# The last two blocks of a fused attention and gated feed-forward kernel: row groups, tokens on partitions, and the casts of the first batch

## The chip, the cores and the metric

The kernel runs on one NeuronCore of one Trainium2 chip. The metric is the time of one execution on the device, in microseconds; the median of three runs is 719.71 us (718.67 to 720.09). The profile is of one execution, with a span of 716.4 us on the core.

Five engines work side by side, each through its own queue in order: TensorE (PE, with its weight loads shown as PEld), VectorE (DVE), ScalarE (ACT), GpSimd (POOL) and SyncE (SP), which here issues the transfers. PE writes its results to PSUM[...]; VectorE and ScalarE read them from there.

## The reference

Four batches of 12416 tokens of 128 channels pass through attention over 32 inducing points, and every token of the result through a gated feed-forward layer with 1536 hidden channels.

```python
def mab(q, kv):
    s = scale * (q @ kv.transpose(0, 2, 1))
    s = s - s.max(-1, keepdims=True)
    a = np.exp(s)
    a /= a.sum(-1, keepdims=True) + 1e-09
    return a @ kv
h = mab(I, x)          # 32 inducing points look at all tokens of the batch
out = mab(x, h)        # each token looks at the 32 points

gate = np.maximum(out @ w_gate, 0.0)
val = out @ w_val
return gate * val @ w_out
```

## The kernel before

Tokens lie as 97 tiles of 128 (`t`) of a batch; a block is four tiles (512 tokens), a pair two blocks, and one tile is left as the rest. `h` never meets the tokens as such: `hgv` holds `h @ w_gate` on partitions 0 to 63 (the 32 rows twice) and `h @ w_val` on 64 to 127, and the unnormalised scores `p2` (exp of the scores, 32 rows per block) multiply it. The sum of the scores is divided out once at the end, squared (`z2i` twice), since gate and value both carry it and the rectifier doesn't mind a positive factor.

A unit is one step of one pair. In a slot of the main loop PE forms the values of an older unit and the gates of the new one, ScalarE rectifies the gates (two of 128x512), VectorE multiplies gate and value (`gv`, one of 128x1024), and PE adds some output steps of a block whose `gv` is done. A pair has 12 units; output jobs stand in a queue, each with a first slot and a count of steps for each of its slots.

```python
    while True:
        unit = next(todo_units, None)
        window.append(unit)
        ready = None if at == 10 else window.pop(0)     # the lag grows by one here
        ...
        def values():
            ready["v"] = bank("v", "v_ps", [P, 2 * BLK])
            for m in ready["mm"][1]:
                form(ready["v"], *m)                     # L830, 32-row matmuls
        if ready and at >= 10:
            values()
        if unit:
            ... gates, L830 ...
        if ready and at < 10:
            values()
        ... posted work, a filler if due, output steps (L640, L696) ...
        if at < 10:
            idle(idle_ps, 2, hgv[:, 0:BLK])
        ... relu on ScalarE (L930), gate * value on VectorE (L933) ...
        at += 1
```

An output step of a regular block has the weights `wo` stationary and 512 tokens moving, so the result has channels on partitions; it is cast to fp16 (L646), transposed by a transfer and scaled on GpSimd (L657). The last two blocks are done otherwise, as the transfer would come too late:

```python
        def step(i):                                     # L696
            nc.tensor.matmul(c["ps"], wo[:, i, :], gv(i), start=(i == 0), stop=(i == NFF - 1))
        def evac(at):
            ... zz = z * z on VectorE (L701) ...
            for a in (0, h):                             # L705
                nc.scalar.copy(out=oT[:, a * P : (a + h) * P], in_=c["ps"][:, a * P : (a + h) * P])
            extra[at + 1].append(lambda: finish(zz, oT, osb))
        def finish(zz, oT, osb):
            for a in (0, h):
                ... transposes on PE (L712), scaling by zz on ScalarE (L716, first block)
                ... or VectorE (L720, last block), store (L727)
```

In the last pair one block's gates use one row group and its values another:

```python
    for r in (32 * k, 64 + 32 * k)     # gates, values of block k; two matmuls each on the same rows
```

The head, for the first batch, takes x in parts of eight tiles (two of four at the end):

```python
    for j in range(n_parts + 3):
        if j < n_parts:                                  # cast to fp16
            h = (t1 - t0) // 2
            nc.gpsimd.tensor_copy(out=dst[:, 0:h, :], in_=x32[:, 0:h, :])       # L283
            nc.scalar.copy(out=dst[:, h:, :], in_=x32[:, h:, :])                # L284
        if 1 < j < n_parts + 2:
            ... scores of part j - 2 on PE (L289), exp on ScalarE (L291)
        if j > 2:
            if j == n_parts + 2:
                nc.tensor.matmul(z1, ones32[0:1, :], z1s[0:1, :], start=False, stop=False)  # L298
            ... sums z1 and hT of part j - 3 on PE (L300, L310, L313)
        if j < n_parts:
            ... transposes of part j on PE (L318), copy to xT on VectorE (L319)
    ... weights cast on GpSimd (L327)
    idle(idle_ps, 3, xT[0][:, 0:4, :].rearrange("p t c -> p (t c)"))            # L272
    hT = finish_h(hT_ps, z1)           # reciprocal L142, product L144 on VectorE
    ... scores of the first pair (L175), hgv (L156, L335, L340), then the main loop
```

`idle` issues matmuls whose results nobody reads.

Of the kernel before, what the change touches and what calls it, by code (L numbers as in the profile page):

```python
# [18 lines left out]
def kernel(  # L19
# [16 lines left out]
    nc = tc.nc  # L36
# [135 lines left out]
    def s2_pair_pe(hT, xT, pr):  # L172
        ps = bank("g", "s2_ps")
        for r in range(4):
            nc.tensor.matmul(  # L175
                ps[32 * r : 32 * r + 32, :],
                hT[:, 0:M],
                xTs(xT, (2 * pr + r % 2) * TPB, TPB),
                start=True,
                stop=True,  # L180
            )
        return ps

    def s2_pair_exp(ps):
        p2 = st([P, BLK], FP16, "p2", 4)
        nc.scalar.activation(out=p2, in_=ps, func=AF.Exp, scale=sm_scale)
        return p2

    def s2_quad_pe(hT, xT, qd):

        ps = bank("g", "s2_ps")
        for r in range(4):
            nc.tensor.matmul(  # L193
                ps[32 * r : 32 * r + 32, :],
                hT[:, 0:M],
                xTs(xT, (4 * qd + r) * TPB, TPB),
                start=True,
                stop=True,
            )
        return ps  # L200
# [6 lines left out]
    def p2_copies(p2q):  # L207

        p2 = [st([P, BLK], FP16, "p2", 4) for _ in range(2)]
# [57 lines left out]
    n_big = n_parts - 2  # L267

# [5 lines left out]
    for j in range(n_parts + 3):  # L274
        if j < n_parts:
# [3 lines left out]
            if t1 == NT:  # L279
                nc.vector.tensor_copy(out=dst, in_=x32)  # L280
            else:
                h = (t1 - t0) // 2
                nc.gpsimd.tensor_copy(out=dst[:, 0:h, :], in_=x32[:, 0:h, :])  # L283
                nc.scalar.copy(out=dst[:, h:, :], in_=x32[:, h:, :])  # L284
# [9 lines left out]
        if j > 2:  # L294
            t0, t1 = parts[j - 3]
            p1, n = p1s[j - 3], t1 - t0
            if j == n_parts + 2:
                nc.tensor.matmul(z1, ones32[0:1, :], z1s[0:1, :], start=False, stop=False)  # L298
            if j - 3 < n_big:
# [31 lines left out]
    s2 = s2_pair_pe(hT, xT, 0)  # L331
    p2 = s2_pair_exp(s2)
# [6 lines left out]
    for k in (1, 2):  # L339
# [33 lines left out]
    def ev_s2_pair(b, pr, first, last):  # L373
        def pe(at):
            ps = s2_pair_pe(state[b]["hT"], state[b]["xT"], pr)

            def act():
                p2s[(b, pr)] = s2_pair_exp(ps)

            post[at + 1].append(act)  # L380
            ev_z2(lambda: p2s[(b, pr)], [(b, pr, k) for k in range(2)], TPB, at + 2)
# [3 lines left out]
    def ev_s2_quad(b, qd, first, last):  # L385
        def pe(at):
            ps = s2_quad_pe(state[b]["hT"], state[b]["xT"], qd)
# [71 lines left out]
    for b in range(B):  # L459
        for qd in range(NPAIR // 2):  # L460
            base = slot(b, 2 * qd, 0)
            if base:

                a = base - 2 * NFF if qd else slot(b - 1, NPAIR, 0) - 14
                ev_s2_quad(b, qd, a + 4, a + 8)
            else:
                ev_s2_pair(b, 1, 5, 8)
# [165 lines left out]
    def chain(w, gv, key, k, t0, first):  # L633
# [43 lines left out]
        if w == BLK:  # L677
            steps = [(first if i == 0 else 0, lambda i=i: step(i)) for i in range(NFF)]
            fast = key[0] == B - 1 and key[1] > NPAIR - 5
            counts = (5, 5) if fast else (6, 5)  # L680
# [6 lines left out]
    extra = defaultdict(list)  # L687

    def last_block(gv, key, k, t0, tag, on_act):
        c = {}  # L690
        h = TPB // 2

        def step(i):
            if i == 0:
                c["ps"] = bank(tag, "o_ps")
            nc.tensor.matmul(c["ps"], wo[:, i, :], gv(i), start=(i == 0), stop=(i == NFF - 1))  # L696

        def evac(at):
            z = z2is[key + (k,)][:, :, 0]
            zz = st([P, TPB], FP32, "zz", 2)  # L700
            nc.vector.tensor_tensor(out=zz, in0=z, in1=z, op=ALU.mult)  # L701
            oT = st([P, BLK], FP16, "oT", 4)
            osb = st([P, TPB, P], FP32, "osb", 4)
            for a in (0, h):
                nc.scalar.copy(out=oT[:, a * P : (a + h) * P], in_=c["ps"][:, a * P : (a + h) * P])  # L705
            extra[at + 1].append(lambda: finish(zz, oT, osb))

        def finish(zz, oT, osb):
            for a in (0, h):
                ps = bank("g", "oo_ps", [P, h, P], FP16)  # L710
                for t in range(h):
                    nc.tensor.transpose(ps[:, t, :], oT[:, (a + t) * P : (a + t + 1) * P], eye16)  # L712
                for t in range(h):
                    sc = zz[:, a + t : a + t + 1]
                    if on_act:
                        nc.scalar.activation(  # L716
# [250 lines left out]
```

The softmax here doesn't subtract the row's maximum and nothing guards it: scores larger than these inputs give would overflow.

## Time and profile before

| what | from the profile |
|---|---|
| span | 716.4 us |
| first gate product of VectorE | starts at 28.67 us |
| last gate product of VectorE | ends at 710.50 us |
| last matmul of an output step | ends at 711.60 us |
| last scaling on VectorE | ends at 713.57 us |

In a list in order of time a row has the start, the duration of what is merged in it, the engine, the line of the kernel, the operation, output and inputs by name, shapes, and a count; brackets tell how long the engine was idle before it and what ended that. Rows of the same kind that follow each other are merged, so the pace of a merged row is its duration less one instruction's, divided by the count less one. A PE row's duration includes the time until its last result is there. The page also gives, by stretches of time, the busy time of each engine and the TensorE clock that was granted.

### The profile page before, as it was taken

What the parts mean: (1) busy time and instruction counts of PE and PEld (TensorE: products, weight loads), DVE (VectorE), ACT (ScalarE), POOL (GpSimd) and SP (SyncE); (2) the same over time, 40 slices, a digit from 0 to 9 for tenths busy, and PEclk for the clock granted to TensorE, in tenths of its full rate; (3) what the DMA queues carried; (4) which work ended last, traced back from release to release, by engine and by line L of the source; (5) the groups of instructions that cost most, each with busy time, mean ns of one, the idle gap of its engine ahead of it and who ended that gap; (6) DMA issues with size and microseconds to landing.
All of it is one profiled execution on the core that took longest, in us unless ns stands there. A gap on an engine that the chain in (4) does not pass through costs nothing.

```text
span 716.4 us, 13907 instructions
## 1 busy us (share of the span) xinstructions
PE 639.5 (89%) x4554; PEld 191.1 (27%) x4554; DVE 684.5 (96%) x630; ACT 679.6 (95%) x1378; POOL 343.3 (48%) x621
## 2 busy tenths in 40 slices
PE   5999999998988999998898999999888898898997
PEld 5422222222222222222222222222222222222222
DVE  4699999999999999999999999999999999999996
ACT  5799999999999999999999999999999999999985
POOL 3574536561365546626163662754325451551531
PEclk9999999999999999999999999999999999999999
DMA  9656677531346978522147766762122133232222
GB/s 344 219 125 177 150 181 163 103 89 45 91 126 166 195 164 223 126 67 76 46 107 206 170 155 170 170 118 75 59 68 83 56 90 67 67 88 67 67 68 72
DMA packets 142489, 87.76 MB, mean 122 GB/s; under 512 B 116913, under 2 KB 125905, under 8 KB 140113
## 3 DMA queue, kind: packets, MB, share of 16 engines
q1 hardware_dynamic: 142416, 86.88, 46.8%
q8 instruction: 35, 0.57, 0.3%
q14 instruction: 38, 0.30, 0.1%
HBM read 27.80 MB, written 25.43 MB: 74 GB/s over the span
## 4 chain that ended last, share of the span: by engine, by line
PE 44%; ACT 23%; issue 15%; DVE 15%; DMA 3%; SPq 0%; POOL 0%; DVEq 0%; ACTq 0%
PE o_ps L640 19%; ACT g L930 16%; DVE gv L933 14%; PE v_ps L830 14%; PE g_ps L830 7%; ACT oT L646 6%; DMA gv<-in_x_dram 2%; PE s_ps L193 1%; PE o_ps L696 1%; PE s1T_ps L511 1%; ACT p1T L521 0%; PE idle_ps L272 0%; DMA p1g<-p1T 0%; ACT hgv L166 0%; PE xT_ps L318 0%
## 5 line engine op out<-in xcount | busy, mean ns | idle before, releaser
L933 DVE TENSOR_TENSOR gv<-g,v_ps 128x1024 f16<-128x1024 f16 x576 | 660.8, 1213 | 10.7 <-PE g_ps L830 6.8
L930 ACT ACTIVATE g<-g_ps 128x512 f16<-128x512 f32 x1164 | 613.3, 620 | 16.6 <-PE g_ps L830 8.6
L640 PE MATMUL o_ps<-gv,wo 128*128 128x512 f16 x1128 | 339.8, 383 | 36.8 <-ACT oT L646 36.6
L657 POOL TENSOR_SCALAR osb<-o,z2i 128x128 f32<-128x128 f16 x380 | 164.6, 447 | 275.0 <-DMA o<-oT 251.3
L830 PE MATMUL g_ps<-p,hgv 32*128 32x512 f16 x1152 | 284.8, 380 | 5.3 <-ACT g L930 1.7
L830 PE MATMUL v_ps<-p,hgv 32*128 32x512 f16 x1152 | 226.2, 383 | 11.5 <-DVE gv L933 9.7
L830 PEld LDWEIGHTS <-hgv 32*128 32x128 f16 x2400 | 73.6, 91 | 271.5 <-issue 267.3
L640 PEld LDWEIGHTS <-wo 128*128 128x128 f16 x1176 | 79.2, 97 | 192.0 <-issue 169.1
L436 POOL TENSOR_TENSOR z2i<-zt,minus 128x16 f32<-128x16 f32 (+2 forms) x29 | 72.5, 2501 | 1.5
L646 ACT CAST oT<-o_ps 128x512 f16<-128x512 f32 (+1 forms) x98 | 57.1, 583 | 0.4 <-PE o_ps L640 0.4
L490 POOL CAST x<-x 128x2048 f16<-128x2048 f32 x18 | 34.0, 1890 | 19.4 <-DMA x<-in_x_dram 15.0
L429 POOL TENSOR_TENSOR zt<-zt 128x128 f32<-128x128 f32 (+5 forms) x116 | 33.4, 288 | 9.1
L595 POOL TENSOR_TENSOR hp<-hp,hq 128x129 f32<-128x129 f32 (+1 forms) x18 | 8.2, 457 | 32.5 <-ACT hq L594 27.9
L429 POOL TENSOR_TENSOR zt<-p2T 128x256 f32<-128x256 f16 (+2 forms) x29 | 17.0, 586 | 9.3 <-DMA p2T<-p2q 7.0
L319 DVE COPY xT<-xT_ps 128x1024 f16<-128x1024 f16 (+1 forms) x13 | 8.5, 650 | 7.2 <-PE xT_ps L318 6.4
L204 ACT ACTIVATE p2q<-s_ps 128x512 f16<-128x512 f32 x23 | 15.1, 656 | 0.0
L283 POOL CAST x<-gv 128x512 f16<-128x512 f32 (+1 forms) x13 | 7.5, 580 | 12.3 <-DMA gv<-in_x_dram 12.2
L284 ACT CAST x<-gv 128x512 f16<-128x512 f32 (+1 forms) x13 | 7.5, 580 | 6.1 <-DMA gv<-in_x_dram 6.1
L521 ACT ACTIVATE p1T<-s1T_ps 128x512 f16<-128x512 f32 x18 | 12.2, 677 | 0.0
L318 PE MATMUL xT_ps<-eye,x 128*128 128x128 f16 x97 | 9.6, 256 | 2.1 <-POOL x L283 1.5
L193 PE MATMUL s_ps<-xT,hT 128*32 128x512 f16 x92 | 9.2, 387 | 1.9
L291 ACT ACTIVATE p<-s_ps 128x256 f16<-128x256 f32 (+2 forms) x14 | 5.0, 354 | 4.9 <-PE s_ps L289 4.8
(90 smaller groups left out, 162.1 us busy)
## 6 DMA issues: line engine op xcount, KB each, us to landing
out_dram<-osb SPq DMA_DIRECT2D x94, 256.0 KB, 2.2
x<-in_x_dram SPq DMA_DIRECT2D x18, 1024.0 KB, 5.8
p<-p2q SPq DMA_DIRECT2D x92, 64.0 KB, 2.0
gv<-in_x_dram SPq DMA_DIRECT2D x11, 512.0 KB, 7.5
o<-oT SPq DMA_TRANSPOSE x98, 2.3
x<-in_moe_w_out_dram SPq DMA_DIRECT2D x1, 768.0 KB, 9.1
gv<-in_x_dram SPq DMA_DIRECT2D x2, 256.0 KB, 10.7
x<-in_moe_w_gate_dram SPq DMA_DIRECT2D x1, 512.0 KB, 9.2
```

What stands on the lines that cost most here:

```text
L193: nc.tensor.matmul(ps[32 * r : 32 * r + 32, :], hT[:, 0:M], xTs(xT, (4 * qd + r) * TPB, TPB), start=True, stop=True,)
L204: nc.scalar.activation(out=p2q, in_=ps, func=AF.Exp, scale=sm_scale)
L429: nc.gpsimd.tensor_tensor(out=dst, in0=v[:, :, :, 0:m], in1=v[:, :, :, m : 2 * m], op=ALU.add)
L436: nc.gpsimd.tensor_tensor(out=z2i, in0=v[:, :, :, 0], in1=minus1[:, 0 : n * g].rearrange("p (n g) -> p n g", n=n), op=ALU.pow,)
L490: nc.gpsimd.tensor_copy(out=s["x16"][:, t0:t1, :], in_=s["x32", q])
L521: nc.scalar.activation(out=p1T, in_=ps, func=AF.Exp, scale=sm_scale)
L640: nc.tensor.matmul(c["ps"][:, 0:w], wo[:, i, :], gv(i), start=(i == 0), stop=(i == NFF - 1))
L646: nc.scalar.copy(out=oT[:, 0:w], in_=c["ps"][:, 0:w])
L657: nc.gpsimd.tensor_scalar(out=osb[:, t, :], in0=o16[:, t, :], scalar1=zz, scalar2=zz, op0=ALU.mult, op1=ALU.mult,)
L830: nc.tensor.matmul(ps[:, cols], hgv[:, s * P : (s + 1) * P], p2, start=True, stop=True)
L930: nc.scalar.activation(out=g16[:, k * BLK : (k + 1) * BLK], in_=ps, func=AF.Relu)
L933: nc.vector.tensor_tensor(out=ready["dst"], in0=ready["g16"][:, 0:n], in1=ready["v"][:, 0:n], op=ALU.mult)
```

## The change

Most of it is for the last pair. All four row groups are used at once: gates of both halves on groups 0 and 1, values on 2 and 3. For that each of the last two blocks gets scores of its own in all four groups, and the pair before gets its scores directly rather than by copies between partitions. The output steps put the tokens on partitions, with `gv` stationary and `wo` moving, so no transpose is needed; four such groups share a bank, which a matmul of zeros opens. The last block is scaled by VectorE straight from PSUM, the one before by GpSimd after a copy by ScalarE. The last gate product is split in two.

```diff
+                if b == B - 1 and qd == NPAIR // 2 - 1:
+                    bl = 2 * NPAIR - 4
+                    ev_s2(b, (b, 2 * qd), (bl, bl + 1, bl, bl + 1), a + 4, a + 8)
+                    for k in range(2):
+                        ev_s2(b, (b, 2 * qd + 1, k), (bl + 2 + k,) * 4, a + 16 + 6 * k, a + 20 + 6 * k)
+                else:
+                    ev_s2_quad(b, qd, a + 4, a + 8)
...
-            counts = (5, 5) if fast else (6, 5)
+            counts = (6, 5)
+            if fast:
+                counts = (4, 4) if (key[1], k) == (NPAIR - 2, 1) else (5, 5)
...
         def step(i):
             if i == 0:
-                c["ps"] = bank(tag, "o_ps")
-            nc.tensor.matmul(c["ps"], wo[:, i, :], gv(i), start=(i == 0), stop=(i == NFF - 1))
+                ps = bank("o", "o_ps")
+                nc.tensor.matmul(ps, zero16, wo[0:1, 0:TPB, :], start=True, stop=False)
+                c["ps"] = ps.rearrange("p (t c) -> p t c", t=TPB)
+            for t in range(TPB):
+                nc.tensor.matmul(
+                    c["ps"][:, t, :],
+                    gv(i)[:, t * P : (t + 1) * P],
+                    wo[:, i, :],
+                    start=False,
+                    stop=(i == NFF - 1 and t == TPB - 1),
+                )
 
         def evac(at):
...
+            if last:
+                h = TPB // 2
+                for a in (0, h):
+                    nc.vector.tensor_tensor(
+                        out=osb[:, a : a + h, :],
+                        in0=c["ps"][:, a : a + h, :],
+                        in1=zz[0][:, a : a + h, :].broadcast_to([P, h, P]),
+                        op=ALU.mult,
+                    )
+                    nc.sync.dma_start(
+                        out=ov[key[0]][:, t0 + a : t0 + a + h, :], in_=osb[:, a : a + h, :]
+                    )
+                return
+            o32 = st([P, TPB, P], FP32, "o32", 1)
+            nc.scalar.copy(out=o32, in_=c["ps"])
+            for t in range(TPB):
+                nc.gpsimd.tensor_scalar(...)
...
-                        if k == 0:
-                            steps = [(base + 8, lambda i=i, f=step: f(i)) for i in range(NFF)]
-                            job(steps, evac, ([3, 3, 3, 3],) * 2)
-                        else:
-                            for i in range(NFF):
-                                a = base + 12 + (i + 2) // 4
-                                extra[a].append(lambda i=i, f=step: f(i))
-                            extra[base + 15].append(lambda f=evac: f(base + 16))
+                            lambda i, k=k: base + 3 + 6 * k + i // 2,      # first slot of step i
+                        job(steps, evac, ([1, 3, 3, 3, 3] if k == 0 else [0] + [4] * 8,) * 2)
...
-                                    for d in range(2)
+                                    for d, r in ((0, 64 * j), (1, 64 * j + 32))
                                 ]
-                                for r in (32 * k, 64 + 32 * k)
+                                for j in range(2)
                             ],
                             dst=gvs[k][:, u % 6, :, :].rearrange("p k c -> p (k c)"),
+                            parts=2 if u == NFF - 1 else 1,
```

The rest is for the head. A full part of x is cast whole by one engine, in turn; only the last part is still shared. Three idle matmuls are added ahead of the last part's sums, to keep PE in work. The lag of the main loop grows at slot 4, and values come ahead of gates throughout. Buffers for `p2` go from four to five, and each of the second and third copies of `hgv` is issued beside its matmuls.

```diff
+            elif j == n_parts - 1:
+                nc.gpsimd.tensor_copy(out=dst[:, 0:2, :], in_=x32[:, 0:2, :])
+                nc.scalar.copy(out=dst[:, 2:4, :], in_=x32[:, 2:4, :])
             else:
-                h = (t1 - t0) // 2
-                nc.gpsimd.tensor_copy(out=dst[:, 0:h, :], in_=x32[:, 0:h, :])
-                nc.scalar.copy(out=dst[:, h:, :], in_=x32[:, h:, :])
+                if on_act:
+                    nc.scalar.copy(out=dst, in_=x32)
+                else:
+                    nc.gpsimd.tensor_copy(out=dst, in_=x32)
+                on_act = not on_act
...
                 nc.tensor.matmul(z1, ones32[0:1, :], z1s[0:1, :], start=False, stop=False)
+                idle(idle_ps, 3, xT[0][:, 0:4, :].rearrange("p t c -> p (t c)"))
...
-        ready = None if at == 10 else window.pop(0)
+        ready = None if at == 4 else window.pop(0)
```

## The prediction

> **What bounds the kernel now.** I read the page's busy times first, then the engines' busy time by stretches, then VectorE alone in order of time, and last the order of time of all engines at the two ends, because the change touches only the first 30 us, a few scores at slots 541 to 563, and the last 20 us.
>
> ```profile
> PE 639.5 (89%) x4554; PEld 191.1 (27%) x4554; DVE 684.5 (96%) x630; ACT 679.6 (95%) x1378; POOL 343.3 (48%) x621
> ```
>
> VectorE (DVE) and ScalarE (ACT) are both nearly full. VectorE alone, late in the last batch:
>
> ```profile
> 638.99 53.25 DVE L933 TENSOR_TENSOR gv<-g,v_ps 128x1024 f16<-128x1024 f16 x47
> ```
>
> 47 gate products without a pause: one lasts 1.22 us and they start every (53.25 - 1.22) / 46 = 1.131 us, so their rate is the floor of a slot here. In batches 0 to 2 six slots take about 7.07 us (the ScalarE evacuations of `oT` at 51.00, 58.06, 65.13) and ScalarE shows almost no pause, so there it sets the rate and VectorE has 7.07 - 6 x 1.131 = 0.28 us in six slots to spare.
>
> PE in that part, one slot from 663.25 to 664.33, and PE, VectorE, ScalarE and the store queue in the last 12 units:
>
> ```profile
> 663.25 0.39 PE L830 MATMUL v_ps<-p,hgv 32*128 32x512 f16 x2
> ...
> 663.58 0.82 PE L640 MATMUL o_ps<-gv,wo 128*128 128x512 f16 x3
> 664.33 0.39 PE L830 MATMUL v_ps<-p,hgv 32*128 32x512 f16 x2
> ```
>
> ```profile
> 695.16 8.75 DVE L933 TENSOR_TENSOR gv<-g,v_ps 128x1024 f16<-128x1024 f16 x7 [0.78 <-ACT g L930]
> ...
> 706.14 0.38 PE L830 MATMUL v_ps<-p,hgv 32*128 32x512 f16 x1
> 706.15 0.38 PE L830 MATMUL g_ps<-p,hgv 32*128 32x512 f16 x1
> 706.37 0.37 PE L830 MATMUL v_ps<-p,hgv 32*128 32x512 f16 x1
> 706.38 0.37 PE L830 MATMUL g_ps<-p,hgv 32*128 32x512 f16 x1
> ...
> 706.68 0.82 PE L696 MATMUL o_ps<-gv,wo 128*128 128x512 f16 x3
> ...
> 710.14 1.46 PE L696 MATMUL o_ps<-gv,wo 128*128 128x512 f16 x6
> ...
> 712.44 1.13 DVE L720 TENSOR_SCALAR osb<-oo_ps,zz 128x128 f32<-128x128 f16 x4 [1.87 <-PE oo_ps L712]
> 713.08 0.85 SPq L727 DMA_DIRECT2D out_dram<-osb  x2
> ```
>
> A regular slot with three output steps takes PE 664.33 - 663.25 = 1.08 us, one of the last units 1.29 us (706.14 to 707.44): there the two matmuls of each side sit in the same row group and follow each other by 0.22 us. So in the last 12 units PE is the bound: VectorE starts every (8.75 - 1.22) / 6 = 1.255 us. After VectorE's last gate product (710.50) there follow 1.10 us of PE, then a ScalarE cast, a transpose, VectorE's scaling (to 713.57) and 2.83 us of store: 5.9 us.
>
> The head:
>
> ```profile
> 19.42 1.09 POOL L283 CAST x<-gv 128x512 f16<-128x512 f32 x2 [0.70 <-DMA gv<-in_x_dram]
> ...
> 20.09 1.03 PE L318 MATMUL xT_ps<-eye,x 128*128 128x128 f16 x8 [0.19 <-POOL x L283]
> ...
> 25.10 0.36 DVE L142 RECIPROCAL rz<-z_ps 128x32 f32<-128x32 f32 x1 [1.05 <-PE hT_ps L313]
> ```
>
> Until 19.4 the casts wait for x; from 20.09 to 23.8 PE has work without a break at a granted clock of 0.50 to 0.56 (the stretches 20 to 23 us), full again from 24. PE is what ends last there.
>
> [...] clock 0.50 after PE's pauses at 17.5 to 18.8, for about 3.4 us; eight warm transposes take 0.61 us, (0.61 - 0.22) / 7 = 56 ns each. [...] here 1024 elements take 1.21 us and 512 take 0.68, so about 1.03 ns an element plus 0.15.
>
> **The change part by part.**
>
> 1. Row groups of the last pair. Gates on groups 0 and 1, values on 2 and 3, all at once. Per slot 1.29 - 1.08 = 0.21 us of PE. The pair needs its own scores: three score groups in place of one for the last four blocks, so two more exps (0.48 us of ScalarE each, by start to start) and eight more matmuls, in slots where VectorE is the bound and PE waits 0.4 to 0.6 us for it every six slots; I put 0.1 us on the path. The partition copies that fall away were hidden.
>
> 2. Output steps as four 128-column matmuls with the tokens on partitions: 4 x 56 = 0.224 us in place of 0.216, nothing. The zero matmul adds 0.22 us per block.
>
> 3. The order of the steps. I stepped the schedule through, with 1.08 us for a slot of three steps, 0.22 us for each step more or fewer, and VectorE at 1.13 us. Slot 578 starts at 694.47 as before. With four steps in slots 579 and 580, all twelve steps of the pair before are done at 698.5 (before, 699.5), the rest block's twelve narrow steps are done at 700.5, the first of the two blocks starts at 701.1 after its bank is evacuated, and ends in slot 587 at about 705.7. From there VectorE is the bound: it is at 705.7 for unit 9, 706.8 for unit 10, and 707.96 for unit 11, whose two halves end at 708.64 and 709.25. Values of unit 11 are formed at 706.9 to 707.2, then PE runs the zero matmul and all twelve steps in a row: 707.2 + 0.22 + 12 x 0.224 = 710.1, plus 0.17 until the last result is there: 710.27. Before it is 711.60. That is 1.35 us earlier, and PE, not the split gate product, ends last.
>
> 4. After the last matmul: before, cast, transpose and scaling take 713.57 - 711.60 = 1.97 us. Now two products of 128x256 from PSUM, 0.15 + 256 x 1.03 ns = 0.41 us each, 0.8 us: 1.15 us less. The store is the same 128 KB per half, 2.83 us from the last product to the end. The first block's scaling on GpSimd (four at about 0.45 us from 706.6) and the rest block's store lie ahead of it. Sum of the tail: -1.35 - 1.15 = -2.5 us.
>
> 5. The head's casts. A part on one engine takes 1.04 us (the weights' 128x1024 cast on GpSimd) in place of 0.61, half as often. Throughput doesn't matter, as x arrives every 1.3 us; the latency of the last full part does: at 19.42 + 1.04 rather than 20.03, 0.4 us later for the transposes that open PE's unbroken stretch. Part of this moves work behind the end of the slow clock at about 23.7, so I charge 0.25 us.
>
> 6. Three idle matmuls ahead of the last part's sums: PE has no pause there (23.8 to 24.9), so 3 x 0.216 = 0.65 us on the path to `hT`. The three behind them ran in VectorE's time (reciprocal and product, 25.10 to 25.80) and still do.
>
> 7. The lag grows at slot 4 rather than 10. VectorE is then 0.5 us ahead less: unit 3's values come at about 32.55 against its readiness at 32.06. This gap falls into the part where ScalarE sets the rate and VectorE regains 0.28 us in six slots, so most of it vanishes: 0.15 us.
>
> 8. The interleaved `hgv` copies keep each engine's order: 0. A fifth `p2` buffer: no wait for one is seen, 0.
>
> Sum: -2.5 + 0.1 + 0.25 + 0.65 + 0.15 = -1.35 us, from 719.71 to 718.4. The two charges on the head are taken at their worst, so I go a little below: 718.1.
>
> **The rivals.**
> - The head costs nothing: the idle matmuls keep PE's clock from falling again, or exp of the last part comes later than PE and they hide behind it. For it: in the profile PE runs at half clock just before. Against: exp ends at 24.42, PE is only free at 24.72. It would make 717.2.
> - The head eats the tail's gain: with whole-part casts PE pauses longer (16.9 to 19.1), and the slow clock lasts over the idle matmuls and `hgv`; then they cost 1.3 us in place of 0.65, and the rest more. [...] That would give 719.5 to 720.
> - The tail gains less, as the twelve steps bunched at the end, or a wait of the scaling for the whole bank rather than its half (0.1 us), keep PE the bound; or the four-step slots hold up the gates and so VectorE. Up to 1 us less: 719.
> - The pauses of VectorE ahead of the last pair (0.26 and 0.78 us) vanish too, since values come 0.2 us earlier: up to 0.5 us more.
>
> **Range and chances.** The three times before span 1.4 us, the head is uncertain by about 0.7 and the tail by 0.8: 716.4 to 719.9. Two per cent is 14.4 us, more than all that is touched at both ends could give; so within 2% is all but sure.
>
> **What would show it.** In the last units VectorE starts every 1.13 to 1.15 us rather than 1.255; a slot of three steps takes PE about 1.09; the twelve last steps run unbroken; from the last matmul to the end 3.7 us rather than 4.8. In the head the first gate product starts at 29.3 to 29.8 rather than 28.67, of which 0.65 is in three matmuls ahead of the last sums, and VectorE pauses once by about 0.5 us near unit 3. I am wrong if the first gate product comes no later, if PE's clock in the head differs, or if the batches between move by more than 0.3 us against each other.

## The result: 0.4% slower, and where it came from

The changed kernel takes 721.66 us (median of six runs, 721.0 to 722.87), the kernel before beside it 719.12 us (718.05 to 720.09): ratio 1.0038, with a 95% interval of 1.0024 to 1.0052. The prediction was 718.1 us, range 716.4 to 719.9. Over the 22 runs of e1 below, and at equal clock, the loss is 1.4 us, or 0.2%; by the fit below, some 0.8 of the 2.5 us here lie in the clock that these few runs were granted. The profiled span went from 716.4 to 719.3 us, so the trace shows the loss.

The page's busy times (first line of the profile after) are nearly those of before. They don't tell what happened:

```profile
PE 640.1 (89%) x4631; PEld 195.3 (27%) x4631; DVE 684.5 (95%) x627; ACT 678.2 (94%) x1367; POOL 348.5 (48%) x633
```

I cut both traces at events that both kernels have, all on VectorE. For before and after, in us:

| stretch | before | after | change |
|---|---|---|---|
| start to the product that makes `hT` | 25.57 | 26.35 | +0.78 |
| from there to the first gate product | 3.10 | 4.28 | +1.18 |
| first to 35th gate product | 39.38 | 40.21 | +0.83 |
| 35th to the first full product of the last batch | 474.71 | 474.65 | -0.06 |
| from there to the rest's first product | 149.40 | 151.69 | +2.29 |
| from there to the end of the last gate product | 18.34 | 17.28 | -1.06 |
| from there to the end of VectorE | 3.07 | 1.98 | -1.09 |
| from there to the end | 2.83 | 2.86 | +0.03 |

The first row mixes several things (in this trace the clock became full only at 16.4 us, in the one of before at 9.9: eight transposes take 1.01 us at 15.12 us and 0.61 at 16.59 here, 1.01 at 8.93 and 0.61 at 11.67 there), so the experiments have to part them. The tail gained about what was predicted. The head lost three times as much as predicted, and the last batch lost 2.29 us where 0.1 was predicted. The changed kernel's VectorE in order of time (start, duration, engine, line, operation, count, and in brackets the idle time before it and what ended that):

```profile
26.35 0.22 DVE L144 TENSOR_TENSOR hT<-hT_ps,rz 128x64 f16<-128x64 f32 x1
...
30.63 3.48 DVE L943 TENSOR_TENSOR gv<-g,v_ps 128x1024 f16<-128x1024 f16 x3 [0.79 <-ACT g L938]
34.90 1.22 DVE L943 TENSOR_TENSOR gv<-g,v_ps 128x1024 f16<-128x1024 f16 x1 [0.79 <-PE g_ps L845]
36.37 34.26 DVE L943 TENSOR_TENSOR gv<-g,v_ps 128x1024 f16<-128x1024 f16 x30 [0.25 <-PE g_ps L845]
...
672.86 1.22 DVE L943 TENSOR_TENSOR gv<-g,v_ps 128x1024 f16<-128x1024 f16 x1 [0.51 <-PE g_ps L845]
674.80 5.93 DVE L943 TENSOR_TENSOR gv<-g,v_ps 128x1024 f16<-128x1024 f16 x5 [0.72 <-PE g_ps L845]
681.05 5.78 DVE L943 TENSOR_TENSOR gv<-g,v_ps 128x1024 f16<-128x1024 f16 x5 [0.32 <-PE g_ps L845]
...
701.40 13.06 DVE L943 TENSOR_TENSOR gv<-g,v_ps 128x1024 f16<-128x1024 f16 x12 [0.20 <-PE g_ps L845]
715.68 0.76 DVE L720 TENSOR_TENSOR osb<-o_ps,zz 128x256 f32<-128x256 f32 x2 [1.21 <-issue]
```

Two pauses, 0.79 and 0.25 us, stand at the fourth and fifth product, and more between 672 and 681 us, where before had 47 products without a pause. The row of twelve holds ten whole products and the two halves of the last (0.68 us each, overlapping to 1.27): a whole one starts every (13.06 - 1.27) / 10 = 1.18 us on average, against 1.255 before. The predicted 1.13 to 1.15 us are the pace of most of them; in the slots with four output steps, PE takes 1.30 us (702.20 to 703.50) and VectorE follows it.

PE in the same trace, at the end:

```profile
707.04 0.39 PE L845 MATMUL v_ps<-p,hgv 32*128 32x512 f16 x2
...
707.37 0.84 PE L706 MATMUL o_ps<-wo,gv 128*128 128x128 f16 x12
...
708.14 0.39 PE L845 MATMUL v_ps<-p,hgv 32*128 32x512 f16 x2
...
712.43 0.37 PE L703 MATMUL o_ps<-wo,zero 1*128 1x512 f16 x1
...
712.73 2.85 PE L706 MATMUL o_ps<-wo,gv 128*128 128x128 f16 x48
```

A slot of three steps takes 708.14 - 707.04 = 1.10 us, where the last units took 1.29; the last block's 48 matmuls run in one piece to 715.58, and the two scalings (0.76 us, row above) follow at once.

And the head, all engines, where the reader should look at the bracket of the third row:

```profile
24.86 0.82 PE L260 MATMUL idle_ps<-xT,eye 128*128 128x512 f16 x3
...
27.97 0.68 DVE L333 CAST hgv<-hgv_ps 128x512 f16<-128x512 f32 x1
28.70 0.39 PE L156 MATMUL hgv_ps<-wg,hT 128*32 128x512 f16 x2 [1.24 <-DVE hgv L333]
...
29.04 0.39 PE L845 MATMUL g_ps<-p,hgv 32*128 32x512 f16 x2
```

PE waits 1.24 us for VectorE's copy of the second third of `hgv` before it writes the last third, and the first gates stand behind that.

### The profile page after: what moved, and what is told of

It is laid out like the page before. It is cut to its first block, busy times and chain, and to the rows that moved or that the text cites. A ratio compares the mean times of both kernels' runs of the same rounds, so it can differ in the third digit from the quotient of the medians.

```text
span 719.3 us, 14051 instructions
## 1 busy us (share of the span) xinstructions
PE 640.1 (89%) x4631; PEld 195.3 (27%) x4631; DVE 684.5 (95%) x627; ACT 678.2 (94%) x1367; POOL 348.5 (48%) x633
## 4 chain that ended last, share of the span: by engine, by line
PE 43%; ACT 23%; DVE 16%; issue 16%; DMA 1%; SPq 0%; POOL 0%; DVEq 0%; ACTq 0%
PE o_ps L643 19%; ACT g L938 16%; DVE gv L943 15%; PE v_ps L845 13%; PE g_ps L845 6%; ACT oT L649 6%; PE s_ps L175 1%; DMA gv<-in_x_dram 1%; PE xT_ps L312 1%; PE s1T_ps L514 1%; PE idle_ps L260 0%; PE o_ps L706 0%; ACT p1T L524 0%; ACT hgv L166 0%; PE s_ps L282 0%
## 5 line engine op out<-in xcount | busy, mean ns | idle before, releaser
L432 POOL TENSOR_TENSOR z2i<-zt,minus 128x16 f32<-128x16 f32 (+3 forms) x31 | 73.4, 2368 | 1.5
L425 POOL TENSOR_TENSOR zt<-zt 128x32 f32<-128x32 f32 (+5 forms) x124 | 35.1, 283 | 9.7
L425 POOL TENSOR_TENSOR zt<-p2T 128x256 f32<-128x256 f16 (+3 forms) x31 | 17.5, 566 | 16.1 <-DMA p2T<-p 8.1
L175 PE MATMUL s_ps<-xT,hT 128*32 128x512 f16 x108 | 10.8, 387 | 2.5
L276 POOL CAST x<-gv 128x1024 f16<-128x1024 f32 x6 | 6.2, 1042 | 12.7 <-DMA gv<-in_x_dram 12.7
L943 DVE TENSOR_TENSOR gvr<-g,v_ps 128x512 f16<-128x512 f16 x12 | 7.9, 684 | 1.5 <-PE g_ps L845 1.5
```

What stands on the lines that cost most here:

```text
L175: nc.tensor.matmul(ps[32 * r : 32 * r + 32, :], hT[:, 0:M], xTs(xT, blocks[r] * TPB, TPB), start=True, stop=True,)
L425: nc.gpsimd.tensor_tensor(out=dst, in0=v[:, :, :, 0:m], in1=v[:, :, :, m : 2 * m], op=ALU.add)
L432: nc.gpsimd.tensor_tensor(out=z2i, in0=v[:, :, :, 0], in1=minus1[:, 0 : n * g].rearrange("p (n g) -> p n g", n=n), op=ALU.pow,)
L943: nc.vector.tensor_tensor(out=ready["dst"][:, a : a + w], in0=ready["g16"][:, a : a + w], in1=ready["v"][:, a : a + w], op=ALU.mult,)
```

## The experiments

All edits are to the changed kernel. The mean granted TensorE clock of each run is known too, and a run takes longer the lower it is: a least-squares fit over all runs, one constant for each kernel and one slope for all, gives 0.45 us for each 0.001 of mean clock, with a scatter of 0.52 us. So I give two times: the median, and the fit's constant, which is the kernel's time at full clock. Runs with a mean clock under 0.993 occur in the kernel before alone (28 of 212, up to 728 us; none of the 239 of all other kernels, and why is open): they are left out of the fit, but not of the ratios, and draw those of e1 to e12 down, that of e1 to 1.0003. The ratio and interval are against the kernel before, run beside each.

| kernel | runs | median us | ratio to before (95%) | at full clock | mean clock lost |
|---|---|---|---|---|---|
| before | 184 | | | 718.43 | 0.0021 |
| changed, first runs | 6 | 721.66 | 1.0038 (1.0024 to 1.0052) | 720.11 | 0.0038 |
| e1 the same again | 22 | 721.35 | 1.0003 (0.9984 to 1.0021) | 719.83 | 0.0032 |
| e2 `hgv` order | 22 | 719.24 | 0.9980 (0.9962 to 0.9999) | 718.58 | 0.0021 |
| e3 scores by copy | 22 | 720.17 | 0.9985 (0.9964 to 1.0006) | 718.93 | 0.0031 |
| e4 tail only | 19 | 717.18 | 0.9942 (0.9921 to 0.9964) | 715.91 | 0.0028 |
| e5 lag at 10 | 20 | 720.12 | 0.9998 (0.9982 to 1.0014) | 719.00 | 0.0023 |
| e6 no added idle | 12 | 720.52 | 0.9996 (0.9971 to 1.0022) | 719.04 | 0.0028 |
| e7 tail, scores direct | 22 | 718.79 | 0.9979 (0.9962 to 0.9997) | 716.80 | 0.0041 |
| e8 tail, free bank | 21 | 716.61 | 0.9948 (0.9931 to 0.9964) | 715.37 | 0.0026 |
| e9 scores in an empty slot | 14 | 716.69 | 0.9974 (0.9963 to 0.9986) | 716.20 | 0.0021 |
| e10 two tiles for `hgv` | 12 | 719.82 | 1.0007 (0.9991 to 1.0024) | 718.42 | 0.0032 |
| e11 casts and tail | 22 | 717.68 | 0.9978 (0.9970 to 0.9986) | 716.46 | 0.0026 |
| e12 as e7, two exps left out | 20 | 718.14 | 0.9971 (0.9952 to 0.9990) | 716.88 | 0.0030 |
| e13 as e9, two exps left out | 5 | 716.39 | 0.9963 (0.9947 to 0.9980) | 714.96 | 0.0030 |

The standard error of a constant is about 0.1 us (0.16 to 0.24 for twelve runs and fewer); the trace stretches below repeat to 0.02 us where the clock is full.

**e1_same.** No edit; the base for the others.

> The changed kernel again, nothing altered. Base for the others: 721.7 us. In its first profile the TensorE clock was at half speed from 671.9 to about 675.4 us, where the scores of the last blocks stand. Theory A (the direct scores bring it about): it is there again at the same place, and VectorE pauses by 0.5 and 0.7 us there. Theory B (chance[...]): absent or elsewhere, and then the span is about 1.3 us shorter, 718.0.

From `hT` on every stretch of its trace is that of the first (4.28, 40.21, 474.70, 151.71 us). The clock was halved again at the same place, from 672.1 us, as theory A has it. The median lies 1.46 us above that of the 72 runs of before beside it; that the first six runs lay 2.5 apart is in part chance in the clock.

**e2_hgv_order.** The copies follow the matmuls again:

```diff
     for k in (1, 2):
         hgv_pe(hT, k, ps[:, (k - 1) * BLK : k * BLK])
+    for k in (1, 2):
         nc.vector.tensor_copy(
```

> Changed kernel, only the loop of the second and third hgv copies undone: both sets of matmuls are issued ahead of both copies, as before. Theory A (in the changed order PE waits 1.24 us for the copy of the other half of the same tile, and the first gates stand behind that wait): the first gate product starts 1.2 us sooner, 29.4 rather than 30.63, and the whole is 1.2 us faster, about 720.4. Rival (the wait is hidden, because ScalarE sets the rate in the batches that follow): first product sooner, but the whole unchanged within 0.3 us, 721.5.

From `hT` to the first gate product 3.03 us rather than 4.28, the first to the 35th product still takes 40.21 us, and the time at full clock falls by 1.25 us. So the order, which I had put at 0, is the largest single loss.

**e3_scores_by_copy.** The last quad's scores are made once and spread by partition copies, as before:

```diff
+                for g in range(4):
+                    nc.sync.dma_start(
+                        out=p2[32 * g : 32 * g + 32, :], in_=q[64 + 32 * k : 96 + 32 * k, :]
+                    )
...
-                if b == B - 1 and qd == NPAIR // 2 - 1:
+                if False:
```

> Changed kernel, only the scores of the last four blocks undone: one score group and one exp as before, and the four row groups of each of the last two blocks are filled by copies between partitions (eight transfers). Theory A (the two more score groups on PE and exps on ScalarE, in slots where VectorE is the bound, cost the 2.2 us that the changed kernel loses between 640 and 697): VectorE runs without a pause there, 719.5. Theory B (most of it is the halved clock and that is chance): about 0.8 us faster on the median, 720.9, and the pauses come and go with the clock.

The last batch's stretch is back at 149.40 us, and the time at full clock falls by 0.90: near the 0.8 us of theory B and far from the 2.2 of theory A, which counted the halved clock in. The trace's fourth stretch grew to 475.95 us: VectorE runs without a pause from 71.57 to 86.80 us and then has four, of 0.47, 0.27, 0.35 and 0.37 us, by 94.4. From these and the run's mean clock of 0.996 I estimate that the clock halved there, at 86 us; the last section comes back to such halvings.

**e4_tail_only.** Everything undone but the last pair's row groups, output form and order (the edits of e2, e3, e5, e6 and the casts in halves).

> Kernel before with only the tail of the change: head as before (casts in halves, no added idle matmuls, hgv loop, lag at slot 10), scores of the last four blocks by copies; the row groups, the token-wise output steps, their order, and the scaling from PSUM are those of the changed kernel. Theory A (the tail alone gains 2.1 us from the rest units to the end): 717.0, ratio 0.997. Rival (the gain of the tail is only the removal of a lateness that the head and the scores had put there): 719, ratio 1.000.

715.91 us at full clock, 2.52 less than before, with 17.31 and 1.96 us for the last two stretches of VectorE: 2.14 us of the gain are there. Another 0.28 lies outside the trace, as device time exceeds the span by 1.95 us here and by 2.23 before.

**e5_lag_at_10.** The lag grows where it did:

```diff
-        ready = None if at == 4 else window.pop(0)
+        ready = None if at == 10 else window.pop(0)
```

with values after gates until then, as before.

> Changed kernel, only the lag of the main loop undone: it grows at slot 10 again, and until then gates come ahead of values. In the traces so far the time from the first gate product to the 35th is 39.38 us in the kernel before and 40.21 in the changed one, every time. Theory A (the missing values of slot 4 leave VectorE without work in a part where VectorE itself sets the rate, and it never makes up for more than a third of it): 39.4 us again, the first gate product at the same time as in the changed kernel, the whole 0.8 us faster. Rival (as predicted: ScalarE sets the rate after slot 11, and the pause is made up; the 0.83 us come from something else): 40.2 stays.

First to 35th product: 39.37 us, against 40.21; 0.83 us less at full clock. Why the two pauses aren't made up shows ScalarE in order of time, here of e5 and then of the changed kernel:

```profile
36.48 9.93 ACT L943 ACTIVATE g<-g_ps 128x512 f16<-128x512 f32 x20
46.28 0.60 ACT L649 CAST oT<-o_ps 128x512 f16<-128x512 f32 x1
```

```profile
36.34 10.77 ACT L938 ACTIVATE g<-g_ps 128x512 f16<-128x512 f32 x20
46.99 0.59 ACT L649 CAST oT<-o_ps 128x512 f16<-128x512 f32 x1
```

In these ten slots there is no evacuation yet, so ScalarE needs only (9.93 - 0.65) / 9.5 = 0.98 us for a slot, less than VectorE's 1.13. It runs ahead of VectorE here and sets the rate afterwards. Where VectorE comes late, ScalarE can't run ahead: its 20 gates take 0.84 us longer, and of the lead that it lacks almost nothing is regained. The edit undoes two things at once, the slot at which the lag grows and the order of values and gates; that it is the lag is read from where the pauses stand, at the fourth and fifth product, and no run parts the two.

**e6_no_added_idle.** The three added matmuls are gone:

```diff
                 nc.tensor.matmul(z1, ones32[0:1, :], z1s[0:1, :], start=False, stop=False)
-                idle(idle_ps, 3, xT[0][:, 0:4, :].rearrange("p t c -> p (t c)"))
```

> Changed kernel without the three idle matmuls ahead of the last part's sums. Theory A (they lie on the path in full): from the end of the last exp of the head to the product that makes hT 0.65 us less, the first gate product at about 30.1, the whole 0.65 us faster. Rival (they keep PE's clock up, which without them is halved while hT, the scores and hgv are formed): the clock column falls to 0.5 between 25 and 29 us and the first gate product is no earlier than 30.6.

From the start of the last exp of the head to VectorE's reciprocal 24.30 - 23.45 = 0.85 us; with the three matmuls (e2) 25.65 - 24.15 = 1.50. The difference is 0.65, as predicted (0.79 by the times at full clock). The clock column of e6 is 1.00 from 20 to 34 us, without the three matmuls, so the rival falls. The last exps and the reciprocals in e6 and in e2, with the waits for PE in brackets:

```profile
23.45 0.28 ACT L284 ACTIVATE p<-s_ps 128x128 f16<-128x128 f32 x1 [0.40 <-PE s_ps L282]
...
24.30 0.36 DVE L142 RECIPROCAL rz<-z_ps 128x32 f32<-128x32 f32 x1 [1.05 <-PE hT_ps L306]
```

```profile
24.15 0.28 ACT L284 ACTIVATE p<-s_ps 128x128 f16<-128x128 f32 x1 [0.40 <-PE s_ps L282]
...
25.65 0.36 DVE L142 RECIPROCAL rz<-z_ps 128x32 f32<-128x32 f32 x1 [1.70 <-PE hT_ps L307]
```

**e7_tail_direct.** As e4, but with the direct scores.

> Kernel before with the tail of the change and with the scores of the last four blocks formed directly, as the change does it (three score groups and three exps in place of one and eight copies). Against e4_tail_only this shows the cost of the direct scores by themselves. Theory A (0.9 us, as in e2, where the clock stayed full; the 1.4 us beyond that in two profiles of the changed kernel were a halved clock, which falls in other places in other kernels): from the first full product of the last batch to the rest's first 150.3 us rather than 149.4, the whole 0.9 us slower than e4, 718.1. Theory B (the direct scores bring the halved clock with them): 151.7 and 719.4, with the clock column at 0.5 near 670.

716.80 at full clock, 0.89 over e4: the direct scores cost the same here as in e3. But its trace has 151.69 us for the last batch, with the clock halved from 669.9 us, as theory B has it, and its mean clock is the lowest of all (0.0041 lost), so its median lies 1.6 us over that of e4. So theory A holds for the cost of the scores, and "falls in other places in other kernels" does not hold for the halving.

**e8_free_bank.** As e4, and the last block's outputs use a bank (a PSUM tile of 128x512 fp32) that the gates have left, so they can begin one slot sooner:

```diff
-                ps = bank("o", "o_ps")
+                ps = bank("g" if last else "o", "o_ps")
...
-                        job(steps, evac, ([1, 3, 3, 3, 3] if k == 0 else [0] + [4] * 8,) * 2)
+                        job(steps, evac, ([1, 3, 3, 3, 3] if k == 0 else [4] * 8,) * 2)
```

> e4_tail_only with one thing more: the last block's output gathers in a bank that the gates have left, rather than in the bank that the block before must vacate, and starts one slot sooner, at four steps a slot. Theory (in the changed kernel twelve steps run in a row behind the last values, and PE ends 1.1 us after VectorE's last gate product; spread so, only the last two steps are left): the last matmul 0.5 us after the last gate product, the whole 0.6 us faster than e4, 716.6, ratio to before 0.9955. Rival (PE was not what ended last; the last gate product and the store are): no change against e4.

PE of e8 at the end:

```profile
708.08 0.38 PE L713 MATMUL o_ps<-wo,zero 1*128 1x512 f16 x1
708.40 1.07 PE L716 MATMUL o_ps<-wo,gv 128*128 128x128 f16 x16
709.40 0.39 PE L855 MATMUL v_ps<-p,hgv 32*128 32x512 f16 x2
709.72 2.06 PE L716 MATMUL o_ps<-wo,gv 128*128 128x128 f16 x32
```

The zero matmul and a third of the steps now lie ahead of the last values, and from the last gate product to the end of VectorE it takes 1.31 us rather than 1.96 (e4). At full clock 0.54 less than e4. This is the fastest of the kernels that compute everything: 718.43 - 715.37 = 3.1 us less than before at full clock, and 4.5 less than the changed kernel (e1).

**e9_empty_slot.** As e7 with e8's bank, and the two blocks' scores sooner. The edit moves the first slot allowed by one; in the trace the four matmuls then stand two slots sooner, where PE has no output steps, as the bank of those is being evacuated:

```diff
-                        ev_s2(b, (b, 2 * qd + 1, k), (bl + 2 + k,) * 4, a + 16 + 6 * k, a + 20 + 6 * k)
+                        ev_s2(b, (b, 2 * qd + 1, k), (bl + 2 + k,) * 4, a + 15 + 6 * k, a + 20 + 6 * k)
```

> e8_free_bank, but with the scores formed directly as in the change, and the two score groups of the last pair issued two slots sooner, in the slots that have no output steps and in which PE waits 0.4 to 0.6 us for VectorE. Theory A (it is the place that costs: in the change each group stands in a slot with two output steps, which becomes 1.71 us long rather than 1.19, two slots after PE had waited; in the empty slot it takes the place of the wait): from the first full product of the last batch to the rest's first 149.5 us, 0.8 less than with the change's placing (150.29 with the clock full), the whole as e8, 716.6. Rival (the extra exps on ScalarE cost, wherever they stand): 150.2, and 717.4. A halved clock in this stretch would add 1.0 to 1.4 us to either.

That doesn't help, and theory A falls: 150.29 us for the last batch, as in e2, and 716.20 at full clock, 0.60 less than e7, of which the bank alone gave 0.54 in e8.

**e10_two_tiles.** The order of the changed kernel, but each third of `hgv` in a PSUM tile of its own:

```diff
-    ps = bank("v", "hgv_ps", [P, 2 * BLK])
     for k in (1, 2):
-        hgv_pe(hT, k, ps[:, (k - 1) * BLK : k * BLK])
+        ps = bank("v", "hgv_ps", [P, 2 * BLK])
+        hgv_pe(hT, k, ps[:, 0:BLK])
...
```

> Changed kernel, the interleaved order of hgv kept, but its second and third part in two PSUM tiles rather than in the halves of one. Theory A (PE's wait of 1.24 us is for the reading of the other half, as the two halves are one tile to the waits): the wait is gone, from the product that makes hT to the first gate product 3.0 us rather than 4.28, the whole 1.2 us faster than the changed kernel, 720.2. Rival (the order itself makes PE wait, whatever the tiles): 4.28 stays.

PE of e10:

```profile
26.88 0.38 PE L156 MATMUL hgv_ps<-wg,hT 128*32 128x512 f16 x2
...
27.38 0.39 PE L843 MATMUL g_ps<-p,hgv 32*128 32x512 f16 x2
```

The bracket is gone and 3.02 us are left from `hT` to the first gate product. So it isn't the order in itself: in the changed kernel, writing one half of the shared tile waited 1.24 us for the reading of the other half.

**e11_casts_and_tail.** As e4 with the casts of whole parts; only the casts differ.

> e4_tail_only with the casts of the change: full parts cast whole, by GpSimd and ScalarE in turn. From the last part's cast on GpSimd to the last exp of the head the traces have 2.63 and 2.65 us with halves and 3.07 with whole parts where nothing else differs. Theory A (the later cast of the last full part delays PE by its 0.43 us): 3.07 again, and the product that makes hT 0.4 us later against the arrival of x; the first gate product moves by less, as it also waits for the weights (0.26 and 0.79 us in e4 and e8): the whole 0.1 to 0.4 us slower than e4. Rival (the clock in the head decides, and casts don't matter): 2.65.

716.46 at full clock, 0.55 over e4. By the trace 3.07 us pass from GpSimd's cast of the last part to the last exp, where halves take 2.63: 0.44. Its first gate product comes no later (27.95 against 28.35), since in this one trace of e4 PE waited 0.26 us for GpSimd's cast of `wv`, which waits for the transfer of the weights (0.54 us in e4; in e8, with the same head, 1.08, and PE 0.79). One trace of each would have said that the casts are free.

**e12_scores_no_exp, e13_empty_slot_no_exp.** e7 and e9 with the exps of the last two blocks left out: both blocks use another pair's scores, so their outputs are not those of the reference. They show what the exps cost, on ScalarE alone.

```diff
-                p2s[key] = s2_exp(ps)
+                p2s[key] = p2s[(b, NPAIR - 2)] if len(key) == 3 else s2_exp(ps)
```

> e7_tail_direct without the exps of the last pair's two score groups: their matmuls are issued as in the change, but nothing reads them, and the last two blocks are formed with the scores of the pair before (so their outputs are left wrong; this kernel is for its time alone). Theory A (ScalarE has no pause in this stretch and starts its evacuations of oT every 6.68 us, 7.17 with an exp between; the 0.89 us are the two exps): from the first full product of the last batch to the rest's first 149.4 us, as with the copies. Rival (the score matmuls, or the bank of PSUM that each score group holds, cost it): 150.0 or more, with the clock full. A halved clock there adds 1.0 to 1.4 us to either.

> e9_empty_slot without the exps of the last pair's two score groups (their matmuls are issued and not read; the last two blocks are formed with the scores of the pair before and are left wrong; for its time alone). So far: groups in slots with output steps and exps, 150.29 us in this stretch; the same without exps, 150.13; groups in the empty slots with exps, 150.29; neither groups nor exps (copies), 149.40. Theory A (two costs, one behind the other: in a full slot a group costs PE's 0.5 us, which hides the exp; in an empty slot PE's part is free and the exp's 0.48 us shows): free of both, 149.4 to 149.5. Rival (the PSUM bank that a group holds keeps the gates waiting, wherever it stands and whatever reads it): 150.0 or more.

The last batch takes 150.13 us in e12, 149.40 in e13: the empty slot alone doesn't help (e9), leaving out the exps alone hardly does (e12, whose theory A falls), both together remove the cost. That also rules out a cost of the bank that a group holds wherever it stands, as e13's groups hold theirs too. (e13 has five runs; that it lies 1.24 us under e9 at full clock, and 0.89 by the trace, is within their error.)

What the four matmuls do to PE's slot show e4 (copies) and e2 (direct scores), each from one slot's values to the next's:

```profile
675.17 0.39 PE L855 MATMUL v_ps<-p,hgv 32*128 32x512 f16 x2
...
675.83 0.61 PE L653 MATMUL o_ps<-gv,wo 128*128 128x512 f16 x2
676.36 0.39 PE L855 MATMUL v_ps<-p,hgv 32*128 32x512 f16 x2
```

```profile
668.84 0.39 PE L846 MATMUL v_ps<-p,hgv 32*128 32x512 f16 x2
...
669.68 0.40 PE L175 MATMUL s_ps<-xT,hT 128*32 128x512 f16 x4
670.02 0.61 PE L644 MATMUL o_ps<-gv,wo 128*128 128x512 f16 x2
670.55 0.39 PE L846 MATMUL v_ps<-p,hgv 32*128 32x512 f16 x2
```

The slot grows from 1.19 to 1.71 us. ScalarE in the last batch, first e2 (scores in the full slot), then e12, then e9, then e13:

```profile
667.07 0.59 ACT L650 CAST oT<-o_ps 128x512 f16<-128x512 f32 x1
667.53 3.08 ACT L939 ACTIVATE g<-g_ps 128x512 f16<-128x512 f32 x6
670.40 0.70 ACT L186 ACTIVATE p<-s_ps 128x512 f16<-128x512 f32 x1
671.02 3.33 ACT L939 ACTIVATE g<-g_ps 128x512 f16<-128x512 f32 x6
674.24 0.59 ACT L650 CAST oT<-o_ps 128x512 f16<-128x512 f32 x1
```

```profile
666.85 0.59 ACT L644 CAST oT<-o_ps 128x512 f16<-128x512 f32 x1
667.32 3.08 ACT L938 ACTIVATE g<-g_ps 128x512 f16<-128x512 f32 x6
670.80 3.25 ACT L938 ACTIVATE g<-g_ps 128x512 f16<-128x512 f32 x6 [0.41 <-PE g_ps L840]
673.94 0.59 ACT L644 CAST oT<-o_ps 128x512 f16<-128x512 f32 x1
```

```profile
665.50 0.59 ACT L644 CAST oT<-o_ps 128x512 f16<-128x512 f32 x1
...
666.93 0.64 ACT L186 ACTIVATE p<-s_ps 128x512 f16<-128x512 f32 x1
667.41 5.37 ACT L938 ACTIVATE g<-g_ps 128x512 f16<-128x512 f32 x10
672.66 0.59 ACT L644 CAST oT<-o_ps 128x512 f16<-128x512 f32 x1
```

```profile
665.26 0.59 ACT L644 CAST oT<-o_ps 128x512 f16<-128x512 f32 x1
665.73 6.33 ACT L938 ACTIVATE g<-g_ps 128x512 f16<-128x512 f32 x12
671.94 0.59 ACT L644 CAST oT<-o_ps 128x512 f16<-128x512 f32 x1
```

From evacuation to evacuation, six slots: 674.24 - 667.07 = 7.17 us with the scores, 7.09 in e12, 7.16 in e9, 6.68 in e13 (before has the same 6.68). VectorE's six products take 6 x 1.131 = 6.79 us, so without the scores it sets the rate, and with them it has to wait. In e12 ScalarE is free of the exp and pauses 0.41 us in its place, because PE needs the slot for four more matmuls. In e9 PE does them in a slot where it has time, and the exp's half microsecond shows instead. PE and ScalarE both lack the half microsecond, so taking it from one leaves it on the other.

## Why the prediction was wrong, step by step

**Step 8, the interleaved `hgv` copies, put at 0: the step that failed most.** I looked only at the order within each engine. That was right and not enough: the copy of one half and the matmuls of the other share a tile, and PE waited 1.24 us for VectorE. Cost 1.25 us (e2), and none with two tiles (e10).

**Step 1, the scores, put at 0.1 us.** I argued that VectorE is the bound there and PE waits for it, so that two exps and eight matmuls would fit. They don't: ScalarE shows no pause either, and each of the two PE slots that take four of the eight matmuls grows by half a microsecond (1.19 to 1.71 us). 0.9 us (e3, e7 against e4), by two costs that stand in for each other (e12, e13). The row groups' 0.21 us a slot, in the same step, was right: 1.10 against a predicted 1.09 us.

**Step 7, the lag, put at 0.15.** The pauses came (0.79 and 0.25 us where one of 0.5 was predicted), but "most of it vanishes" failed: until the output steps begin VectorE itself is the slowest engine, and its pause becomes ScalarE's. 0.83 us (e5).

**Steps 3 and 4, the tail, put at -2.5.** The trace gives -2.12 (the last three rows of the first table). Step 4 stands: from the last matmul to the last scaling 0.86 us rather than 1.97, so 1.11 of 1.15. Step 3 was too large: the last matmul ends 1.04 us earlier against the rest's first product, not 1.35, because the first of the two blocks began 0.29 us later than put (9.23 us after the rest's first product, not 8.94: PE waited 0.28 us for ScalarE to evacuate its bank), VectorE reached unit 9 0.2 us later, and PE's last piece ended 1.12 us after the last gate product, not 1.02. (The zero matmul of step 2 took 0.30 us, 712.43 to 712.73, rather than 0.22.) That PE and not the split product ends last was right. That the times at full clock give 2.52 us for the tail (e4), the very number put, is luck: 0.28 of it lies outside the trace, in a term that the prediction didn't have.

**Steps 5 and 6.** Idle matmuls 0.65 of 0.65 (e6). Casts 0.44 by trace and 0.55 by time, where 0.25 was put: the latency of 0.4 was right, and no part of it moved behind a slow clock.

At full clock these parts add up to 1.25 + 0.90 + 0.83 + 0.79 + 0.55 - 2.52 = +1.80 us; measured is 719.83 - 718.43 = +1.40 for e1. The difference of 0.4 us is no more than the error of such a sum of constants. The head's four parts cost 3.42 us one by one, and together 719.83 - 716.80 = 3.03 (e1 against e7): some overlap is possible, but not shown. On top, e1 lost 0.0011 more of its clock than before, 0.5 us. Together +1.9, the difference of the means of the runs in the fit.

**The rivals.** "The head costs nothing" falls: the idle matmuls cost 0.65 us, and the clock was full without them (e6). "The head eats the tail's gain" named nearly the right size, but by a slow clock over the idle matmuls and `hgv`; in the trace it is full there, from 16.4 us on. "The tail gains less" holds for 0.3 of its 1 us. The pauses ahead of the last pair didn't vanish: 0.26 and 0.57 us and a new one of 0.20, where 0.26 and 0.78 were. Two signs of being wrong that the prediction had named did appear: PE's clock in the head differs (full from 16.4 us on, rather than from 9.9, and not halved at 20 to 23), and the last batch moved by 2.29 us against those before it.

## What to carry to other kernels

Before calling a reordering free, look for a tile that two engines share: here the wait went by the tile, not by the half that was used (1.24 us with one tile, none with two). Where two engines are as close to full as PE and ScalarE are here (89% and 94% of the span), look at both before adding work to either: two exps and eight matmuls cost 0.89 us, and leaving the exps out gave back 0.16 us of it (e12), moving the matmuls to an empty slot nothing (e9). Nor count on a pause being made up: here the engine that set the later rate was held up meanwhile, and 0.83 us stayed (e5). A change of many parts is better taken apart at once: here the tail alone was worth 2.5 us, and the parts that came with it cost more.

## What was not expected of the hardware

PE's clock halves in the middle of steady work, for 3.4 us each time by the clock columns. The changed kernel by stretches of 2 us (busy time and count of PE, PEld, DVE, ACT and POOL, granted clock, DMA share, GB/s):

```profile
668.00:670.00 2.00, 1.33 (x11) 0.26 (x9) 2.00 (x2) 2.00 (x6) 0.00 (x0) 1.00 0.00 0
670.00:672.00 2.00, 1.88 (x12) 0.44 (x11) 2.00 (x3) 2.00 (x6) 0.46 (x2) 0.94 0.58 174
672.00:674.00 2.00, 2.00 (x8) 0.39 (x7) 1.49 (x2) 1.62 (x4) 1.29 (x3) 0.50 0.19 55
674.00:676.00 2.00, 2.00 (x13) 0.54 (x13) 1.28 (x2) 1.09 (x2) 0.87 (x4) 0.71 0.04 9
```

VectorE and ScalarE are short of work while it lasts, and it costs 151.69 - 150.29 = 1.4 us against e2, whose last batch has the same work at full clock. That is the other part of the 2.29 us in the first table. The clock records give 3.413 us for this halving and for the one at 20.1 us of the kernel before. The full clock ahead of it lasts 655.36 us here and 10.24 us there. The same kernel has a halving in some runs only (ten of e2's 22 runs have a mean clock of 1.000). PE was at work for more than half of the time ahead of both. Here it was busy for 3.2 of the 4 us before 672, and for 2.62 of the 3.41 us before the halving. In the kernel before, where the prediction tied the halving to PE's pauses, the longest of these is 1.28 us, and PE was busy for 1.94 of the 3.41 us before. What brings a halving is not known from these runs. Halvings were seen at 82 to 86, 253, 425 to 427, 670 to 672 and 683 to 687 us, the first three at the same place of a batch (53 to 55 us after its first full gate product).

Whether the direct scores bring the one at 670 to 672 us is not settled. For it: it stands in five of the eight profiles with the scores in full slots (the changed kernel, e1, e6, e7, e10; not e2, e5, e12) and in none of the seven others; and e7 lost 0.0013 more of its clock than e4, which differs in the scores alone, 0.6 us. Against it: e1 and e3, which differ in the same, lost equally much. The clock column reads 1.00 also before the first recorded change, but there it can't be relied on: eight transposes of the changed kernel take 1.01 us at 14.0 us and 0.61 at 21.1. Nor is it known why the device time exceeds the span by 2.2 us in the kernel before, by 1.8 in the changed one and all others with direct scores, and by 2.0 in those with the changed tail and copies: by the span the changed kernel loses 0.4 us more than by the device time.
